# First batch's score tiles as two products of 64 rows each, by halves of the keys

## The chip, the cores and the metric

The kernel runs on one core of one Trainium2 chip, as one launch. The metric is the device time of that launch in microseconds (us), the median of several runs. A shorter time is better.

## The reference

Attention over 4 batches of 8 heads, 576 positions and 64 values a head, all in 32-bit floats, with a threshold in the softmax, and then two feed-forward layers over the 2304 tokens:

```python
scores = scale * np.matmul(q, k.transpose(0, 1, 3, 2))
thresh = np.max(scores, axis=-1, keepdims=True) - tau
scores = np.where(scores >= thresh, scores, -1000000000.0)
scores = scores - np.max(scores, axis=-1, keepdims=True)
attn = np.exp(scores)
attn = attn / (np.sum(attn, axis=-1, keepdims=True) + 1e-09)
return np.matmul(attn, v)                 # then, per token:
x = (s * maximum(x @ w_in, 0)**2 + b) @ w_out
h = x @ w2_in;  out = (maximum(h, 0) + alpha * minimum(h, 0)) @ w2_out
```

A change of the last bits of a score can move a position over the threshold, so the first batch's scores are plain 32-bit products.

## The kernel before

**Stages.** Attention of the first batch comes first (0 to about 131 us in the trace). The weights of the first feed-forward layer are unpacked on DVE, ACT and POOL beside it, and from 80 us on the first layer's products fill TensorE's (PE's) gaps. Then come the other three batches beside the first layer (to about 500 us), and last the rest of both layers.

**Heads.** Heads are taken in pairs. The first batch has four pairs (`p < NP`, `whole`, `first` in `pair`). Of each pair q, k and v are loaded with the two heads side by side, so that after a transposition on PE the 128 partitions are 2 heads x 64 values. A pair has nine score tiles of 128 queries x 576 keys: four for each head, and one with the last 64 queries of both heads (`i == NQ`, the tail). Four pairs make 36 tiles, 32 of one head and 4 tails.

**A score tile before.** PE has 128 rows, a head has 64 values. The scaled queries of a head are written with a factor that is zero on the other head's partitions (`sc_h`, line 676 and 678), so that a product over all 128 rows gives one head. A tile is two products (line 742), keys 0 to 287 and 288 to 575, each into a PSUM bank of its own:

```python
nc.tensor.matmul(sp.t[:, x, :HS], lhsT=o[0][:, c], rhs=o[1][:, x * HS:(x + 1) * HS], ...)
```

The trace shows each 32-bit product as two matmul instructions of 288 columns, each with its weight load, so four to a tile. Then DVE takes the row maxima (`mx`, line 752), POOL the threshold (754), ACT the exponentials (`e`, 756), DVE the masked sum (758); PE transposes `e` by chunks of keys (877, 881), ACT copies these to `gf` and `sh` (887), and PE multiplies them with v (852).

**Moves.** What PE has transposed lies in PSUM and is moved to SBUF: before, six moves a pair, k with 512 and with 64 columns (ACT, 668), q with 512 and with 64 columns for each head (DVE or ACT, 676 and 678).

**Order.** Nothing is ordered by hand. Every piece of work is a task with an engine (or several to choose from), a cost, a rank and its buffers; `Plan.run` plays these costs through once and writes down each engine's instructions in the order in which the tasks start there. On the chip each engine goes through its list in that order. So another cost or another task moves instructions on all engines, far behind its own place too. Two PSUM buffers hold scores (`sc`), one bank (`bank3`, `moe_s`) is shared by the transpositions of pairs 1 to 3 and later by the feed-forward layer.

## Time and profile before

| | |
|---|---|
| Median of three runs | 1115.76 us (1115.6 to 1116.54) |
| Span of the profiled execution | 1111.8 us, from its first to its last instruction |
| Between the two | 3.96 us, before the first and behind the last instruction |
| PE, weight loads, DVE, ACT, POOL busy | 98%, 95%, 82%, 68%, 32% of the span |

The profiled execution is known by its span alone; its time as a run is the span and what lies around it. PE has 98% of the span by the page, but a matmul's record goes on behind the last column that it takes in, so records of neighbours overlap, and the rate of PE is read from one start to the next. The granted clock has 1.00 in every slice of the page; the first 14 us show starts at twice the distance of later ones, as at the lower of the two levels.

### The profile page before, as it was taken

Reading aid. Unit: us, or ns where it says so; the run is one execution under the profiler, and the core shown is the slowest. Engines: PE = TensorE matmul, PEld = TensorE weight load, DVE = VectorE, ACT = ScalarE, POOL = GpSimd, SP = SyncE. Lnnn points to the kernel's source line nnn. Section 1 sums busy time; section 2 is a strip of 40 time slices with the busy share of each in tenths; the row PEclk is TensorE's granted clock in tenths of the full one; section 3 lists DMA queues with packets and bytes.
Section 4 is the critical chain, followed back from the end, with each engine's and each line's share of the span. In section 5 each row is a group of like instructions: output and inputs, shape, how many; then the busy total and the mean of one; then the engine's idle time right before and its main releaser. Section 6 shows DMA issues by size and latency. Waiting matters only on the chain.

```text
span 1111.8 us, 22073 instructions
## 1 busy us (share of the span) xinstructions
PE 1090.6 (98%) x7536; PEld 1051.7 (95%) x7536; DVE 911.6 (82%) x2055; ACT 755.5 (68%) x1737; POOL 352.1 (32%) x476
## 2 busy tenths in 40 slices
PE   8999999999999999999999999999999999999998
PEld 7777899998999999999999999999999999999998
DVE  4898888879888988757877789589986999998882
ACT  4888878867877868744554377357786998565551
POOL 1576764644654646500000013020120332112111
PEclk9999999999999999999999999999999999999999
DMA  5663363446444454044466565428834464554531
GB/s 119 177 167 123 107 168 86 109 118 156 109 118 118 118 124 108 12 139 134 125 217 209 173 205 161 126 86 278 279 132 164 146 211 154 159 160 119 154 90 39
DMA packets 185265, 158.36 MB, mean 142 GB/s; under 512 B 72000, under 2 KB 162112, under 8 KB 185152
## 3 DMA queue, kind: packets, MB, share of 16 engines
q1 hardware_dynamic: 182624, 154.79, 48.6%
q10 hardware_dynamic: 2528, 2.16, 0.7%
q8 instruction: 59, 0.97, 0.3%
q14 instruction: 54, 0.44, 0.1%
HBM read 91.10 MB, written 44.56 MB: 122 GB/s over the span
## 4 chain that ended last, share of the span: by engine, by line
PE 79%; DVE 9%; ACT 5%; DMA 3%; issue 2%; SPq 1%; POOL 0%; DVEq 0%; ACTq 0%; POOLq 0%
PE bank L480 12%; PE bank L481 11%; PE bank L482 11%; PE bank_b L481 8%; PE bank_b L480 8%; PE bank_b L482 8%; PE bank L852 7%; PE sc L742 7%; PE bank L877 5%; ACT e L756 1%; PE bank L881 1%; DVE e L758 1%; PE bank L660 1%; DMA stg<-wfi 1%; DVE mx L752 1%
## 5 line engine op out<-in xcount | busy, mean ns | idle before, releaser
L758 DVE SCALAR_TENSOR_TENSOR e<-sc,mx,e 128x576 f32<-128x576 f32 x144 | 116.3, 813 | 16.8 <-ACT e L756 13.2
L756 ACT ACTIVATE e<-sc,mx 128x576 f32<-128x576 f32 x144 | 106.4, 742 | 21.4 <-DVE mx L752 20.7
L877 PE MATMUL bank<-eyes,e 128*128 128x128 f32 (+1 forms) x640 | 120.2, 274 | 0.6 <-ACT gf L896 0.3
L752 DVE TENSOR_REDUCE mx<-sc 128x1 f32<-128x576 f32 x144 | 107.0, 751 | 13.7 <-PE sc L742 12.8
L877 PEld LDWEIGHTS bank<-eyes,e 128*128 128x128 f32 (+1 forms) x640 | 80.2, 139 | 13.4 <-issue 1.3
L480 PE MATMUL bank<-xt,wa 128*128 128x256 f32 (+1 forms) x266 | 84.3, 317 | 1.9 <-ACT rest L518 1.1
L480 PE MATMUL bank<-gt,wa 128*128 128x256 f32 (+1 forms) x267 | 83.5, 313 | 0.9 <-ACT rest L518 0.7
L481 PE MATMUL bank<-gt,wa 128*128 128x256 f32 (+1 forms) x267 | 78.9, 295 | 0.2 <-DVE gt L458 0.2
L482 PE MATMUL bank<-gt,wa 128*128 128x256 f32 (+1 forms) x267 | 78.9, 295 | 0.0
L754 POOL TENSOR_SCALAR mx<-mx,tau_s 128x1 f32<-128x1 f32 x144 | 51.4, 358 | 83.7 <-DVE mx L752 80.2
L482 PE MATMUL bank<-xt,wa 128*128 128x256 f32 (+1 forms) x266 | 76.8, 289 | 0.0
L481 PE MATMUL bank<-xt,wa 128*128 128x256 f32 (+1 forms) x266 | 76.7, 289 | 0.0
L742 PE MATMUL sc<-k,q 128*128 128x288 f32 x272 | 65.5, 369 | 1.8 <-DVE e L758 0.9
L852 PE MATMUL bank<-gl,vt 128*128 128x256 f32 (+1 forms) x192 | 64.8, 338 | 1.2 <-POOL gl L907 0.6
L852 PE MATMUL bank<-gh,vt 128*128 128x256 f32 (+1 forms) x192 | 57.8, 301 | 0.1
L541 ACT ACTIVATE gt<-rest,b_b,s_b 128x384 fp32r<-128x384 f32 x56 | 39.5, 708 | 26.5 <-DVE rest L539 26.3
L481 PE MATMUL bank_b<-gt,wa 128*128 128x384 f32 (+1 forms) x168 | 54.4, 324 | 1.1 <-DVE gt L531 1.0
L912 DVE TENSOR_TENSOR gl<-bank,gh 128x256 fp32r<-128x256 f32 (+1 forms) x96 | 43.4, 452 | 14.3 <-ACT gh L910 12.8
L480 PE MATMUL bank_b<-gt,wa 128*128 128x384 f32 (+1 forms) x168 | 54.3, 323 | 0.2 <-ACT n L1174 0.2
L480 PEld LDWEIGHTS bank<-xt,wa 128*128 128x128 f32 x266 | 50.4, 189 | 4.1 <-ACT rest L518 2.2
L482 PE MATMUL bank_b<-gt,wa 128*128 128x384 f32 (+1 forms) x168 | 54.1, 322 | 0.0
L922 POOL TENSOR_TENSOR gr<-gf,gh 64x256 fp32r<-64x256 f32 (+1 forms) x48 | 39.7, 828 | 44.2 <-DVE gl L920 43.0
(649 smaller groups left out, 4158.2 us busy)
## 6 DMA issues: line engine op xcount, KB each, us to landing
stg<-in_moe_w_in_dram SPq DMA_DIRECT2D x32, 512.0 KB, 4.0
stg<-in_moe_w_out_dram SPq DMA_DIRECT2D x32, 512.0 KB, 3.7
qo<-hq SPq DMA_DIRECT2D x32, 256.0 KB, 4.3
gf<-rest SPq DMA_DIRECT2D x30, 192.0 KB, 2.3
rest<-gf SPq DMA_DIRECT2D x40, 128.0 KB, 2.9
ko<-hk SPq DMA_DIRECT2D x32, 144.0 KB, 2.7
xr<-xs SPq DMA_DIRECT2D x6, 768.0 KB, 5.2
yf<-yb SPq DMA_DIRECT2D x24, 192.0 KB, 2.6
```

The source lines that it names most:

```text
L480: nc.tensor.matmul(o, lhsT=wl, rhs=mh, start=first, stop=False, skip_group_check=on_top)
L481: nc.tensor.matmul(o, lhsT=wh, rhs=ml, start=False, stop=False, skip_group_check=on_top)
L482: nc.tensor.matmul(o, lhsT=wh, rhs=mh, start=False, stop=last, skip_group_check=on_top)
L742: nc.tensor.matmul(sp.t[:, x, :HS], lhsT=o[0][:, c], rhs=o[1][:, x * HS:(x + 1) * HS], start=n == 0, stop=n == len(passes) - 1)
L752: add("DVE", dve(S), lambda sp=sp, mx=mx: nc.vector.tensor_reduce(mx.t[:, 0:1], sp.t[:, :, :HS], op=ALU.max, axis=AX.XY, negate=True), (sp ...
L754: t2 = add("POOL", 0.26, lambda mx=mx: nc.gpsimd.tensor_scalar(mx.t[:, 1:2], mx.t[:, 0:1], -1.0, tau_s, op0=ALU.mult, op1=ALU.subtract), ( ...
L756: add("ACT", act(S, 1), lambda sp=sp, mx=mx, e=e: nc.scalar.activation(halves(e.t), sp.t[:, :, :HS], AF.Exp, bias=mx.t[:, 0:1]), (sp, mx), ...
L758: add("DVE", dve(S) + 0.065, lambda sp=sp, mx=mx, e=e, col=col, sums=sums: nc.vector.scalar_tensor_tensor(halves(e.t), sp.t[:, :, :HS], mx ...
L852: nc.tensor.matmul(o.t[:, :n], lhsT=w.rearrange("p a b -> p (a b)"), rhs=m.t[:, :n], start=c == first and x == 0, stop=c == last and x == ...
L877: nc.tensor.transpose(gt.t[:rows, m:m + P], es[i].t[:, keys], ident)
L912: add("DVE", dve(n), lambda hi=hi, lo=lo, gt=gt: nc.vector.tensor_tensor(lo.t[:, :n], gt.t[:, :n], f32(hi.t[:, :n]), op=ALU.subtract), (gt ...
L922: add("POOL", pool2(n), lambda hi=hi, f=f, hf=hf: nc.gpsimd.tensor_tensor(hi.t[:TL, :n], f.t[:TL, :n], f32(hf.t[:TL, :n]), op=ALU.subtract ...
```

## The change

The keys of the first batch are kept in two halves of 288, and both queries and keys twice: once with head 0 on partitions 0 to 63 and head 1 on 64 to 127 (index 0), once the other way round (index 1). For a tile of head h the product with the first half of the keys then uses the 64 rows on one half of the array, and that with the second half the 64 rows on the other half. The four tails keep products over 128 rows; for these POOL clears the columns where a head has no queries. The order of the keys within `e` changes (0 to 255, 512 to 575, 256 to 511), and the transpositions of `e` read their chunks accordingly.

The moves from PSUM become thirteen a pair: q with 512 columns at once and two more of 64 partitions, k with 256 columns three times (twice 64 partitions) and with 32 columns three times, and four of 64 columns for the tail's queries. Each of them may go to ACT or DVE.

```diff
--- before.py
+++ after.py
@@ -582,7 +582,9 @@
-        q32, k32 = tiles(ep, NP, "q32", [P, NS * P]), tiles(ep, NP, "k32", [P, S])
+        q32, k32 = tiles(ep, NP, "q32", [P, 2, NK * P]), tiles(ep, NP, "k32", [P, 2, HS])
+        for t in q32:
+            nc.gpsimd.memset(t[:, :, NQ * P:], 0.0)
@@ -602,6 +604,48 @@
+        def twice(p, nat, q_of, k_of, rank):
+
+            n = HS - G1
+            tk, tq, tt = (Buf(one_s, "misc"), Buf(one_s, "gt"), Buf(moe_s)) if p == 0 else (Buf(moe_s), Buf(moe_s), Buf(moe_s))
+
+            def turned(t, tr, cs):
+                for i, c in enumerate(cs):
+                    nc.tensor.transpose(tr.t[:, i * P:(i + 1) * P], t.t[:, c].rearrange("p h d -> p (h d)"), ident)
+
+            def move(o, tr, cols, to, by=None, rows=P):
...
+                add([("ACT", act(w, by is not None), rank), ("DVE", dve(w) + 0.065 * (by is not None), rank)], 0, go, (tr,), (to,))
+
+            every, (lo, hi) = slice(0, P), half(0)
+            add("PE", pe(P, NQ), lambda: turned(nat["k"], tk, range(NQ)), (nat["k"],), (tk, k_of), rank=rank)
+            add("PE", pe(P, NQ), lambda: turned(nat["q"], tq, range(NQ)), (nat["q"],), (tq, q_of), rank=rank)
+            move((q32[p][:, 0, :NQ * P], every), tq, slice(0, NQ * P), q_of, sc_p)
+            move((k32[p][:, 0, :G1], every), tk, slice(0, G1), k_of)
+            for a, b in (lo, hi), (hi, lo):
+                move((k32[p][a, 1, n:], b), tk, slice(G1, 2 * G1), k_of)
+            add("PE", pe(P), lambda: turned(nat["k"], tt, (NQ,)), (nat["k"],), (tt, k_of, q_of), rank=rank)
+            move((k32[p][:, 0, G1:], every), tt, slice(0, n), k_of)
+            for a, b in (lo, hi), (hi, lo):
+                move((k32[p][a, 1, :n], b), tt, slice(n, 2 * n), k_of)
+            for a, b in (lo, hi), (hi, lo):
+                move((q32[p][a, 1, :NQ * P], b), tq, slice(0, NQ * P), q_of, sc_p)
+            for h, b in enumerate((lo, hi)):
+                for x, a in enumerate((b, (hi, lo)[h])):
+                    move((q32[p][a, x, NQ * P + h * TL:NQ * P + (h + 1) * TL], b), tt, slice(TL, P), q_of, sc_p)
@@ -643,8 +687,10 @@
+            if first:
+                twice(p, nat, qs[0], ks[0], ready)
+            for nm in () if first else "kq":
...
@@ -663,22 +709,6 @@
-                    if first:
-                        if nm == "k":
-                            add("ACT", act(n), lambda hl=hl, tr=tr, c=c, n=n: nc.scalar.activation(
-                                k32[p][:, c], tr.t[:, :n], AF.Copy), (tr,), (hl,), rank=ready)
-                            continue
-                        for h in range(2):
...
-                            add([("DVE", dve(n) + 0.065, ready), ("ACT", act(n, 1), ready)], 0, scaled, (tr,), (hl,))
-                        continue
@@ -727,14 +757,19 @@
+                    def by_keys(sp=sp, h=h, c=slice(ii * P, (ii + 1) * P)):
+                        for x in range(2):
+                            r = slice(0, P) if h is None else half(h ^ x)[0]
+                            nc.tensor.matmul(sp.t[:, x, :HS], lhsT=q32[p][r, x, c], rhs=k32[p][r, x], start=True, stop=True)
@@ -743,7 +778,7 @@
-                    add("PE", pe(HS, 8) if first else pe_r(HS, 2 * len(passes)), score, of, (sp,), rank=rank - AHEAD)
+                    add("PE", (pe(HS, 8) if h is None else pe(HS, 4) + 0.1) if first else pe_r(HS, 2 * len(passes)), by_keys if first else score, of, (sp,), rank=rank - AHEAD)
@@ -869,7 +904,10 @@
-                keys = slice(S - rows, S) if c == NQ else slice(c * P, (c + 1) * P)
+                if plain:
+                    keys = slice(G1, G1 + rows) if c == NQ else slice(c * P + TL * (c > 1), (c + 1) * P + TL * (c > 1))
+                else:
+                    keys = slice(S - rows, S) if c == NQ else slice(c * P, (c + 1) * P)
```

In the order of the instructions, ACT from its first move on. Before (`q320`, `k320` are queries and keys of pair 0 in SBUF, `bank0` to `bank3` PSUM banks, `[waits X]` names the engine waited for):

```order
L678 ACTIVATE q320_165<-bank0_105,by_half_77 128x512 [waits DVE_49]
L668 ACTIVATE k320_169<-bank2_107 128x512 [waits PE_49]
L668 ACTIVATE k320_169<-bank3_108 128x64 [waits DVE_49,PE_49]
L756 ACTIVATE e0_137<-sc0_109,mx0_154 128x576 [waits DVE_49]
L756 ACTIVATE e1_138<-sc1_110,mx1_155 128x576 [waits DVE_49]
```

and now:

```order
L627 ACTIVATE q320_165<-bank0_105,sc_p_76 64x512 [waits DVE_49]
L627 ACTIVATE q320_165<-bank0_105,sc_p_76 64x512
L623 ACTIVATE k320_169<-bank2_107 64x256 [waits DVE_49]
L623 ACTIVATE k320_169<-bank2_107 64x256
L627 ACTIVATE q320_165<-bank3_108,sc_p_76 64x64 [waits DVE_49,PE_49,Pool_49]
L627 ACTIVATE q320_165<-bank3_108,sc_p_76 64x64 [waits DVE_49]
L791 ACTIVATE e0_137<-sc0_109,mx0_154 128x576 [waits DVE_49]
L791 ACTIVATE e1_138<-sc1_110,mx1_155 128x576 [waits DVE_49]
```

Six moves of pair 0 stand in front of the first exponential on ACT where three stood.

DVE from the first row maximum on, where the second pair's moves (`q321`, `k321`) fall. Before:

```order
L752 TENSOR_REDUCE mx0_154<-sc0_109 128x1 [waits PE_49]
L752 TENSOR_REDUCE mx1_155<-sc1_110 128x1 [waits PE_49]
L758 SCALAR_TENSOR_TENSOR e0_137,sums0_158<-sc0_109,mx0_154,e0_137 128x576 [waits Activation_49,Pool_49]
L676 TENSOR_SCALAR q321_166<-bank3_108,by_half_77 128x512 [waits PE_49]
L758 SCALAR_TENSOR_TENSOR e1_138,sums0_158<-sc1_110,mx1_155,e1_138 128x576 [waits Activation_49,Pool_49]
L752 TENSOR_REDUCE mx2_156<-sc0_109 128x1 [waits PE_49]
L758 SCALAR_TENSOR_TENSOR e2_139,sums0_158<-sc0_109,mx2_156,e2_139 128x576 [waits Activation_49,Pool_49]
L752 TENSOR_REDUCE mx3_157<-sc1_110 128x1 [waits PE_49]
L676 TENSOR_SCALAR q321_166<-bank3_108,by_half_77 128x64 [waits PE_49,Activation_49]
L758 SCALAR_TENSOR_TENSOR e3_140,sums0_158<-sc1_110,mx3_157,e3_140 128x576 [waits Activation_49,Pool_49]
```

and now:

```order
L787 TENSOR_REDUCE mx0_154<-sc0_109 128x1 [waits PE_49]
L787 TENSOR_REDUCE mx1_155<-sc1_110 128x1 [waits PE_49]
L793 SCALAR_TENSOR_TENSOR e0_137,sums0_158<-sc0_109,mx0_154,e0_137 128x576 [waits Activation_49,Pool_49]
L793 SCALAR_TENSOR_TENSOR e1_138,sums0_158<-sc1_110,mx1_155,e1_138 128x576 [waits Activation_49,Pool_49]
L625 TENSOR_SCALAR q321_166<-bank3_108,sc_p_76 64x512 [waits Activation_49]
L787 TENSOR_REDUCE mx2_156<-sc0_109 128x1 [waits PE_49]
L787 TENSOR_REDUCE mx3_157<-sc1_110 128x1 [waits PE_49]
L621 COPY k321_170<-bank3_108 64x256 [waits Activation_49]
L793 SCALAR_TENSOR_TENSOR e2_139,sums0_158<-sc0_109,mx2_156,e2_139 128x576 [waits Pool_49]
L621 COPY k321_170<-bank3_108 64x32 [waits Activation_49]
L625 TENSOR_SCALAR q321_166<-bank3_108,sc_p_76 64x64 [waits Activation_49] x2
L793 SCALAR_TENSOR_TENSOR e3_140,sums0_158<-sc1_110,mx3_157,e3_140 128x576 [waits Pool_49]
```

Two moves of pair 1 have become five, in the same four tiles.

PE in steady work, a score tile (L742, now L770) among the transpositions of `e` (L877, now L915) and the products with v (L852, now L887). Before:

```order
L852 MATMUL bank2_107<-sh0_145,v320_173 128x256 [waits Pool_49]
L877 MATMUL bank0_105<-eyes_70,e0_137 64x128 [waits Activation_49]
L877 MATMUL bank0_105<-eyes_70,e1_138 64x128
L852 MATMUL bank2_107<-gf1_144,v320_173 128x256
L742 MATMUL sc0_109<-k321_170,q321_166 128x288 [waits DVE_49]
L742 MATMUL sc0_109<-k321_170,q321_166 128x288
L852 MATMUL bank2_107<-sh1_146,v320_173 128x256 [waits Activation_49]
```

and now:

```order
L887 MATMUL bank1_106<-sh0_145,v320_177 128x256 [waits Activation_49,Pool_49]
L614 MATMUL bank3_108<-eyes_70,nat2_132 128x128 [waits DMAHW1_49,DMAHW0_49,Activation_49]
L915 MATMUL bank2_107<-eyes_70,e0_137 128x128
L915 MATMUL bank2_107<-eyes_70,e1_138 128x128
L770 MATMUL sc0_109<-k320_169,q320_165 128x288 [waits DVE_49]
L770 MATMUL sc0_109<-k320_169,q320_165 128x288
L887 MATMUL bank1_106<-gf1_144,v320_177 128x256 [waits Activation_49]
L915 MATMUL bank0_105<-eyes_70,e0_137 64x128
L915 MATMUL bank0_105<-eyes_70,e1_138 64x128
L887 MATMUL bank1_106<-sh1_146,v320_177 128x256 [waits Activation_49]
```

The two score products stand next to each other, and products over 128 rows stand in front and behind. In the whole new order the 32 tiles with half the rows stand in 28 such places.

## Rows read from the trace of the kernel before

**Rows 1.** The page, part 1: busy time, share of the span, instructions.

```profile
PE 1090.6 (98%) x7536; PEld 1051.7 (95%) x7536; DVE 911.6 (82%) x2055; ACT 755.5 (68%) x1737; POOL 352.1 (32%) x476
```

**Rows 2.** Busy time by stretch; the first row names the columns.

```profile
core 0: us, PE busy (x) PEld busy (x) DVE busy (x) ACT busy (x) POOL busy (x), PEclk, DMA share, GB/s
0.00:20.00 20.00, 17.09 (x74) 14.30 (x75) 8.27 (x21) 7.42 (x15) 3.84 (x21) 1.00 0.58 131
20.00:80.00 60.00, 57.54 (x306) 44.07 (x305) 49.72 (x112) 49.24 (x117) 33.99 (x44) 1.00 0.64 166
80.00:140.00 60.00, 59.21 (x360) 48.81 (x360) 52.76 (x110) 50.47 (x108) 41.74 (x47) 1.00 0.39 114
140.00:500.00 360.00, 352.13 (x2837) 343.40 (x2836) 298.27 (x698) 269.17 (x608) 186.74 (x275) 1.00 0.45 114
500.00:1111.80 611.80, 604.63 (x3967) 601.07 (x3966) 502.60 (x1117) 379.19 (x892) 85.82 (x93) 1.00 0.52 160
```

**Rows 3.** PE in order of time, in the middle of the stretch.

```profile
61.33 0.38 PE L877 MATMUL bank<-eyes,e 128*128 128x128 f32 x2
61.55 1.14 PE L742 MATMUL sc<-k,q 128*128 128x288 f32 x4
62.52 0.59 PE L852 MATMUL bank<-gf,v 128*128 128x256 f32 x2
```

**Rows 4.** PE in order of time, from the first score tile on.

```profile
9.57 4.21 PE L742 MATMUL sc<-k,q 128*128 128x288 f32 x8 [0.56 <-ACT k L668]
13.57 1.01 PE L828 MATMUL bank<-eyes 128*128 128x128 f32 x4
...
15.36 1.24 PE L742 MATMUL sc<-k,q 128*128 128x288 f32 x4
```

**Rows 5.** Groups by line and shape, 0 to 140 us: score matmuls, moves, nearest copies.

```profile
L742 PE MATMUL sc<-k,q 128*128 128x288 f32 x160 | 46.2, 415 | 1.1 <-ACT k L668 0.6 <-DVE e L758 0.4
...
L887 ACT ACTIVATE gf<-bank 128x256 f32<-128x256 f32 x16 | 6.2, 387 | 3.2 <-PE bank L877 3.2
...
L814 DVE TENSOR_TENSOR z<-z,bank 128x256 f32<-128x256 f32 x8 | 3.4, 420 | 3.5 <-ACT z L934 3.4
...
L676 DVE TENSOR_SCALAR q<-bank,by_half 128x512 f32<-128x512 f32 x4 | 3.0, 750 | 3.9 <-PE bank L660 3.1 <-ACT q L678 0.7
L678 ACT ACTIVATE q<-bank,by_half 128x512 f32<-128x512 f32 x4 | 2.8, 702 | 7.5 <-DVE q L676 7.0 <-PE bank L660 0.5
...
L668 ACT ACTIVATE k<-bank 128x512 f32<-128x512 f32 x4 | 2.4, 601 | 0.0
...
L678 ACT ACTIVATE q<-bank,by_half 128x64 f32<-128x64 f32 x4 | 1.1, 313 | 1.4 <-DVE q L676 1.4
...
L676 DVE TENSOR_SCALAR q<-bank,by_half 128x64 f32<-128x64 f32 x4 | 1.0, 278 | 0.7 <-PE bank L660 0.7
L668 ACT ACTIVATE k<-bank 128x64 f32<-128x64 f32 x4 | 0.9, 224 | 1.1 <-PE bank L660 1.0
```

**Rows 6.** Line 938, an ACT copy from one half of the partitions to the other.

```profile
L938 ACT ACTIVATE sh<-bank x48: 377/407/437, 143.0 to 478.5; 64x256 f32<-64x256 f32 x24, 64x320 f32<-64x320 f32 x24
```

**Rows 7.** ACT in order of time, the moves before the first score.

```profile
8.35 0.69 ACT L678 ACTIVATE q<-bank,by_half 128x512 f32<-128x512 f32 x1 [6.34 <-DVE q L676]
8.93 0.92 ACT L668 ACTIVATE k<-bank 128x512 f32<-128x512 f32 x2
```

**Rows 8.** DVE in order of time, the same stretch.

```profile
7.56 0.75 DVE L676 TENSOR_SCALAR q<-bank,by_half 128x512 f32<-128x512 f32 x1 [3.09 <-PE bank L660]
9.05 0.47 DVE L676 TENSOR_SCALAR q<-bank,by_half 128x64 f32<-128x64 f32 x2 [0.74 <-PE bank L660]
```

**Rows 9.** Waits of 20 to 140 us: total, times, longest.

```profile
DVE e L758 <- ACT e L756: 4.5, 7, 1.1
DVE mx L752 <- PE sc L742: 4.5, 11, 0.9
```

**Rows 10.** Line 480: first and last start of the feed-forward products.

```profile
L480 PE MATMUL bank<-xt,wa x266: 277/283/525, 80.7 to 896.7; 128*128 128x256 f32 x116, 128*128 128x384 f32 x17
```

More of the change, by code (lines that the diff above doesn't have):

```diff
@@ L603, in half, with go @@
             return (slice(0, D), slice(D, P)) if h == 0 else (slice(D, P), slice(0, D))
+        def twice(p, nat, q_of, k_of, rank):
[5 more added lines that the diff above has]
+            def move(o, tr, cols, to, by=None, rows=P):
+                def go(e, o=o):
+                    d, r = o
+                    if by is None:
+                        if e == "DVE":
+                            nc.vector.tensor_copy(d, tr.t[r, cols])
+                        else:
+                            nc.scalar.activation(d, tr.t[r, cols], AF.Copy)
+                    elif e == "DVE":
+                        nc.vector.tensor_scalar(d, tr.t[r, cols], by[r], None, op0=ALU.mult)
+                    else:
+                        nc.scalar.activation(d, tr.t[r, cols], AF.Copy, scale=by[r])
+                w = cols.stop - cols.start
+                add([("ACT", act(w, by is not None), rank), ("DVE", dve(w) + 0.065 * (by is not None), rank)], 0, go, (tr,), (to,))
[15 more added lines that the diff above has]
+                    move((q32[p][a, x, NQ * P + h * TL:NQ * P + (h + 1) * TL], b), tt, slice(TL, P), q_of, sc_p)
@@ L645, in pair @@
             qk, ends = {}, ((sc_h[0], slice(NQ * P, S)), (sc_h[1], slice(S, S + TL)))
-            for nm in "kq":
-                t, hl = nat[nm], (ks if nm == "k" else qs)[0] if first else Buf(hk_s if nm == "k" else hq_s)
+            if first:
+                twice(p, nat, qs[0], ks[0], ready)
+            for nm in () if first else "kq":
+                t, hl = nat[nm], Buf(hk_s if nm == "k" else hq_s)
                 qk[nm] = hl
@@ L655, in pair @@
                     else:
-                        tr = Buf(one_s, {"k": "misc", "q": "gt"}[nm]) if p == 0 and not tail else Buf(moe_s) if whole else Buf(one_s, "misc")
+                        tr = Buf(one_s, "misc")
                         def transpose(t=t, tr=tr, cs=(NQ,) if tail else tuple(range(NQ))):
@@ L729, in pair @@
                     if first:
[L730 removed]
+                        of, passes = (qs[0], ks[0]), ()
                     elif h is None:
@@ L735, in pair, with score @@
                         of, passes = (qs[h], ks[h]), [(qs[h], 1, ks[h], None), (qs[h], 0, ks[h], None)]
-                    def score(sp=sp, passes=passes, c=slice((col if first else ii) * P, ((col if first else ii) + 1) * P)):
+                    def by_keys(sp=sp, h=h, c=slice(ii * P, (ii + 1) * P)):
+                        for x in range(2):
+                            r = slice(0, P) if h is None else half(h ^ x)[0]
+                            nc.tensor.matmul(sp.t[:, x, :HS], lhsT=q32[p][r, x, c], rhs=k32[p][r, x], start=True, stop=True)
+                    def score(sp=sp, passes=passes, c=slice(ii * P, (ii + 1) * P)):
                         for n, o in enumerate(passes):
```

8 lines of the change are left out of this document (1 added, 7 removed).

## The prediction

> **What bounds the kernel now.** I read the busy shares first: PE 98%, DVE 82%, ACT 68%, POOL 32% [rows 1]. A share is a mean over stages, so next the busy time by stretch [rows 2]. From 20 to 140 us, where the first batch runs, PE is busy 57.54 + 59.21 = 116.75 of 120 us, DVE 49.72 + 52.76 = 102.48, ACT 49.24 + 50.47 = 99.71. PE is the bound there with 3.25 us of waits, and DVE is a near second with 17.5 us to spare. Behind it PE stays the bound: 352.13 of 360 us, then 604.63 of 611.8. So what PE saves in the first batch is passed on to the end, since the work behind it is PE's too; from 80.7 us on feed-forward products already stand ready to fill PE [rows 10]. The first 20 us are different: PE has 17.09, DVE 8.27 and ACT 7.42, and there the chain from load to first score decides.
>
> In order of time, a score tile starts at 61.55 and the next product at 62.52: 0.97 us for four matmul instructions, 0.243 each [rows 3]. Its record is 1.14 long, so 0.17 us of tail lie behind the last column taken in. A tile whose weight load started only with it has a record of 1.24 in place of 1.14 [rows 3, 4]: a bare weight load is 0.10 us. The first two tiles run at the lower of TensorE's two levels: eight instructions from 9.57 to 13.57, 0.50 each [rows 4], though the stretch has 1.00 as granted clock [rows 2].
>
> **The change part by part.**
>
> *Score tiles.* 32 of 36 become two products of 64 rows, on different halves of the array. No instruction goes away: two 32-bit products of 288 columns are still four matmul instructions. All the gain is in how far the two run at once, and the trace has no matmul with half the rows (the score group is 128*128 throughout [rows 5]). Bounds for one tile, from rows: two fully abreast, half of 0.97, 0.49 us; nothing abreast, and at both changes of shape the tail of 0.17 and a bare load of 0.10, 0.97 + 2 x 0.27 = 1.51. That is -0.48 to +0.54 us a tile, over 32 tiles -15.4 to +17.3 us.
>
> I take a value between. A product's two instructions need the same 64 rows, so the second waits for the first, and the second product stands behind both in PE's list. If PE starts matmuls in the order of its list, only the last instruction of the first product and the first of the second run together: three steps of 0.243, 0.73 us. I add one bare load of 0.10, for weights that can't be loaded while other shapes occupy the rows. That is 0.83, 0.14 less than 0.97, and nearer to the row of today's tile than to either end: 32 x 0.14 = 4.5 us less on PE.
>
> The Trainium skill ("TensorE: Matmul & The Clock Gate", The mechanism) says that matmuls on different row groups start about 4 ns apart, and that matmuls start and end in the order of the program; the first half by itself would make a tile 0.49 us, both together give the three steps. No run here shows either yet.
>
> *Moves.* Before, a pair has six: 0.60 + 0.22 for k, 2 x 0.73 + 2 x 0.30 for q (means of the DVE and ACT rows), 2.88 us [rows 5]. Now thirteen. Time goes by columns, not partitions: a copy of 64 partitions with 256 columns from one half to the other is 0.377 at its shortest, one over 128 is 0.387 [rows 5, 6], so crossing halves costs nothing. Three scaled ones of 512 are 3 x 0.73 = 2.18, three of 256 columns 3 x 0.39 = 1.17 (on DVE about 0.42, line 814), three of 32 at most as those of 64, 3 x 0.22 = 0.67, four scaled of 64 are 4 x 0.30 = 1.18: 5.20 us. Four pairs: 4 x 2.32 = 9.3 us more, about 4.7 us on each of DVE and ACT. Most of it hides behind PE. But DVE would then have 107.2 of 115.5 us (120 less the 4.5), and its spare time falls from 17.5 to 8.3. PE's 3.25 us of waits grow; I charge half as much again, 1.6 us. If the cover is gone altogether the price is one engine's 4.7, if PE never notices it is nothing. Waits of today between these engines are small: DVE waits 4.5 us for exponentials and 4.5 for scores [rows 9], and a sooner score shortens the second.
>
> *Start.* ACT issues one move of 0.69 from 8.35 and two of k until 9.85 [rows 7], DVE its first from 7.56 [rows 8]. Now ACT has two scaled ones (1.4) and two of 256 columns (0.8) from 8.35, until about 10.5; the first tile's second product needs the last of these. Its first product can start near 9.5, with 0.96 us at the lower level, so the second starts about where it would in any case. The first tile ends where it did, near 11.5, the second up to 0.5 us sooner. Bounds: 0.7 later (10.5 against 9.85), 0.5 sooner; I take nothing. Two moves of pair 1 that become five fall on DVE between row maxima, 0.3 to 0.8 us each; that is in the 1.6.
>
> *At nothing.* Four clearings on POOL fall into the first 20 us, where it is busy 3.84 with 21 instructions [rows 2]; uncovered, at their mean of 0.18, they would cost 0.7. The other order of the keys moves no instruction. Tails stay as they are. The new order behind 140 us moves work everywhere without making any; I take 0, and 2 us to either side as its bounds, a fifth of PE's idle 7.9 us of 140 to 500.
>
> *Sum.* -4.5 + 1.6 = -2.9 us. The profiled span is 1111.8; with 3.96 us around it that execution stands for the median of 1115.76. 1111.8 - 2.9 + 3.96 = **1112.9 us**.
>
> **The rivals.**
>
> 1. *Both products fully abreast.* The four instructions take two steps and a bare load, 0.49 + 0.10 = 0.59: 32 x 0.38 = 12.2 us off PE. For it: the tile's products write two PSUM banks and read different partitions, so nothing shared is seen. Against: PE's rows show strict succession everywhere. DVE would have 107.2 us in 107.8, so some 4 of the 12 come back as waits: -8, **1107.8**.
>
> 2. *Changes of shape cost more than the overlap gives* (the other side). A score tile stands between products over 128 rows; in the new order the 32 tiles stand in 28 such places, so PE changes shape 56 times. If each waits out the tail of 0.17, a tile is 0.73 + 0.34 = 1.07, 32 x 0.10 = 3.2 us more, and with the 1.6 of the moves +4.8; if each has the bare load too, 0.73 + 0.54 = 1.27, +9.6 + 1.6 = +11.2. Time 1120.5 to 1127, middle **1122**. It decides from 0.92 us a tile on, where 32 x 0.05 only pays the 1.6: that is 0.19 us for the two changes. For it: a tail and a bare load can be read in the rows. Against: both are hidden between all other shapes of today, such as 128 and 288 columns [rows 3]. The Trainium skill ("TensorEngine Tiling (Array Packing)", Key Properties) speaks for this rival: changing the tiling mode drains TensorE, changing the tile alone does not. No run here shows such a change yet.
>
> 3. *The change doesn't do what it says:* the halves run one after the other at 0.97. Then only the moves count: +1.6, **1117.4**. Against it: they use different rows.
>
> 4. *PE gains, but the vector engines hand none of it on,* because in the first 20 to 40 us pair after pair waits for 13 moves through one bank: 4.5 saved, 4.7 lost, **1116**. For it: ACT's wait for DVE's move of q is 7.0 us [rows 5], nearly all of it at the start. Against: PE's 57.54 of 60 us.
>
> **How the numbers follow.** Forecast 0.36, rival 1 0.25, rival 2 0.20, rival 3 0.09, rival 4 0.10. The likeliest's own range is 1110 to 1115. The range: up to 1121 it takes in rivals 3 and 4 and the lower part of rival 2, leaving out about 0.12; down to 1106 nearly all of rival 1, leaving out 0.06. About 0.2% (2.2 us) is what a measurement of this kernel can tell from no change. Faster than 1113.5: rival 1's 0.25 and 0.27 of the forecast's 0.36, 0.52. Within 1113.5 to 1118: 0.09 of the forecast and 0.13 of rivals 3 and 4, 0.22. Slower: rival 2's 0.20 and 0.06 of rivals 3 and 4, 0.26.
>
> **What would show it.** The score rows of the first batch must read 64*128; from a tile's first start to the start of the next product is 0.83 (0.59: rival 1; 1.07 or more: rival 2; 0.97: rival 3). Starts within a tile tell the overlap: third start with the second is mine, third with the first is rival 1. The groups of the moves should add up to about 21 us where there were 11.5. In 20 to 140 us PE's waits should grow from 3.25 to about 5; if they grow by as much as PE saves, it was rival 4. I am wrong if the tile is shorter and the span isn't, or if a later stretch moves by more than 2 us.

## The result and the profile after

The changed kernel takes 1127.34 us (median of 4 runs, 1125.95 to 1128.1) against 1115.68 of the kernel before on the same chip: a ratio of 1.0103, interval 1.0089 to 1.0117, so 11.7 us slower. Forecast were 1112.9 and a range up to 1121. Its profiled execution is the run of 1125.95, with a span of 1124.2 us.

The page's first part answers to [rows 1]:

```profile
PE 1091.2 (97%) x7536; PEld 1037.0 (92%) x7536; DVE 923.5 (82%) x2078; ACT 750.7 (67%) x1737; POOL 353.0 (31%) x485
```

The busy time of DVE rose by 11.9 us, and that of PE did not fall. By stretch, for [rows 2]:

```profile
core 0: us, PE busy (x) PEld busy (x) DVE busy (x) ACT busy (x) POOL busy (x), PEclk, DMA share, GB/s
0.00:20.00 20.00, 14.27 (x78) 10.51 (x78) 9.84 (x26) 9.72 (x20) 5.00 (x25) 1.00 0.58 131
20.00:80.00 60.00, 51.51 (x264) 32.62 (x263) 52.57 (x113) 46.05 (x110) 25.09 (x33) 0.94 0.54 138
80.00:140.00 60.00, 57.53 (x338) 41.70 (x336) 49.72 (x105) 49.02 (x104) 38.63 (x45) 1.00 0.41 119
140.00:500.00 360.00, 351.54 (x2797) 339.06 (x2797) 297.45 (x694) 266.19 (x609) 198.06 (x289) 1.00 0.46 112
500.00:1124.20 624.20, 616.37 (x4068) 613.12 (x4066) 513.88 (x1143) 379.72 (x897) 86.18 (x94) 1.00 0.52 160
```

From 20 to 140 us PE is busy 109.04 us, where it was 116.75, so it stands idle 10.96 us where it stood 3.25. That isn't a gain: the work of the first batch ends later, and the first feed-forward product, which [rows 10] have at 80.7, starts at 94.0.

```profile
L480 PE MATMUL bank<-xt,wa x268: 277/283/520, 94.0 to 915.8; 128*128 128x256 f32 x116, 128*128 128x384 f32 x18
```

PE in order of time shows the new score tile (start, length, idle time ahead), to be set against [rows 3]:

```profile
22.62 0.76 PE L770 MATMUL sc<-k,q 64*128 64x288 f32 x4
23.31 0.70 PE L887 MATMUL bank<-gf,v 128*128 128x256 f32 x2
```

From the tile's start to the next product's it is 0.69 us, before 0.97. The records of the single instructions show how: of one tile, two start at 63.278 and 63.285, the other two at 63.625 and 63.632. Two instructions on the same 64 rows start 0.24 us apart where nothing runs abreast (`e16`, below), so each of these pairs has one instruction of either product: the two products run fully abreast.

Most of the 0.28 is lost again at the two changes of shape. Ahead of the tile 0.09 us more pass than elsewhere (shown below). Behind it the first of the next product's two instructions takes 0.32 us, before 0.215; in the rows that product has 0.70, where [rows 3] have 0.59. From the last instruction ahead of a tile to the second one behind it, where nothing waits, 1.21 us pass where 1.30 passed: 0.09 us less a tile, some 3 us over 32.

The Trainium skill ("TensorE: Matmul & The Clock Gate", The mechanism) has matmuls on different rows start some 4 ns apart, and the 7 ns are near that. It also has matmuls start in the order of the program; that can't be read here, since a record doesn't tell which product it belongs to.

The moves by line and shape, 0 to 140 us (count | busy us, mean ns | idle time ahead and what ended it), answer to [rows 5]:

```profile
L770 PE MATMUL sc<-k,q 64*128 64x288 f32 x128 | 25.3, 470 | 2.2 <-DVE e L793 1.8 <-DVE k L621 0.3
...
L627 ACT ACTIVATE q<-bank,sc_p 64x512 f32<-64x512 f32 x6 | 4.1, 682 | 8.1 <-DVE q L625 8.0
...
L627 ACT ACTIVATE q<-bank,sc_p 64x64 f32<-64x64 f32 x9 | 2.8, 309 | 2.4 <-DVE q L625 2.3
...
L623 ACT ACTIVATE k<-bank 64x256 f32<-64x256 f32 x6 | 2.3, 377 | 0.8 <-DVE k L621 0.8
...
L625 DVE TENSOR_SCALAR q<-bank,sc_p 64x64 f32<-64x64 f32 x7 | 2.0, 284 | 3.0 <-ACT q L627 3.0
```

All 14 groups of moves add up to 20.4 us, where there were 11.2. ACT's wide moves wait 8.0 us for DVE's moves of the same queries, but 7.0 of that was there before [rows 5], nearly all of it ahead of the first score. New are the waits of the small moves: DVE's wait 3.0 us for ACT's and ACT's 2.3 for DVE's, where ACT's had waited 1.4 and DVE's none for ACT. One bank's moves go to and fro. The waits of 20 to 140 us (total, times, longest) answer to [rows 9]:

```profile
PEld bank L887 <- ACT gf L925: 10.8, 14, 1.6
...
PE bank L887 <- ACT gf L925: 6.1, 8, 1.3
DVE e L793 <- ACT e L791: 4.6, 7, 1.7
...
DVE mx L787 <- PE sc L770: 3.8, 8, 0.8
```

The two waits of [rows 9] are as they were. New is the first: PE's weight loads (PEld) for the products with the values wait 10.8 us for ACT's copies of the transposed weights (`gf`), before 2.0; PE itself waits 6.1 us for them, before 0.6. Such a row of PEld has to be read with care. Behind a 64-row tile, where nothing else waits, the weight loads stand still for 0.385 us each time (before: 0.05), and the view puts that down to whatever was signalled last (ACT's `e`, `z`, `wa` or `gf`, or nothing). In the changed kernel 4 of the 14 waits for `gf` stand behind a tile, and the other 10 make 8.0 us, so here most of it is waiting for ACT.

### The profile page after: what moved, and what is told of

Its sections match the earlier page's. It is cut to its first block, busy times and chain, and to the rows that moved or that the text cites. A ratio compares the mean times of both kernels' runs of the same rounds, so it can differ in the third digit from the quotient of the medians.

```text
span 1124.2 us, 22112 instructions
## 1 busy us (share of the span) xinstructions
PE 1091.2 (97%) x7536; PEld 1037.0 (92%) x7536; DVE 923.5 (82%) x2078; ACT 750.7 (67%) x1737; POOL 353.0 (31%) x485
## 4 chain that ended last, share of the span: by engine, by line
PE 77%; DVE 9%; ACT 7%; DMA 3%; issue 2%; SPq 1%; POOL 1%; DVEq 0%; ACTq 0%
PE bank L480 11%; PE bank L481 11%; PE bank L482 11%; PE bank_b L481 8%; PE bank_b L480 8%; PE bank_b L482 8%; PE bank L887 6%; PE bank L915 5%; PE sc L777 4%; PE sc L770 1%; ACT e L791 1%; PE bank L919 1%; DVE mx L787 1%; DVE e L793 1%; DMA stg<-xs 1%
## 5 line engine op out<-in xcount | busy, mean ns | idle before, releaser
L915 PE MATMUL bank<-eyes,e 128*128 128x128 f32 (+1 forms) x640 | 121.4, 276 | 3.3 <-DVE e L793 0.8
L791 ACT ACTIVATE e<-sc,mx 128x576 f32<-128x576 f32 x144 | 106.0, 742 | 11.7 <-DVE mx L787 10.7
L915 PEld LDWEIGHTS bank<-eyes,e 128*128 128x128 f32 (+1 forms) x640 | 79.7, 139 | 20.6 <-ACT gf L941 1.7
L480 PE MATMUL bank<-gt,wa 128*128 128x256 f32 (+1 forms) x258 | 79.8, 309 | 0.2
L481 PE MATMUL bank<-gt,wa 128*128 128x256 f32 (+1 forms) x258 | 76.0, 294 | 0.3 <-DVE gt L458 0.3
L482 PE MATMUL bank<-gt,wa 128*128 128x256 f32 (+1 forms) x258 | 75.9, 294 | 0.0
L789 POOL TENSOR_SCALAR mx<-mx,tau_s 128x1 f32<-128x1 f32 x144 | 47.0, 327 | 87.7 <-DVE mx L787 75.2
L887 PE MATMUL bank<-gl,vt 128*128 128x256 f32 (+1 forms) x192 | 65.6, 342 | 0.7 <-POOL gl L945 0.6
L887 PE MATMUL bank<-gh,vt 128*128 128x256 f32 (+1 forms) x192 | 58.2, 304 | 0.9 <-DVE z L977 0.6
L481 PE MATMUL bank_b<-gt,wa 128*128 128x384 f32 (+1 forms) x177 | 57.4, 324 | 1.0 <-DVE gt L531 1.0
L480 PE MATMUL bank_b<-gt,wa 128*128 128x384 f32 (+1 forms) x177 | 57.3, 324 | 0.5 <-ACT gt L530 0.5
L482 PE MATMUL bank_b<-gt,wa 128*128 128x384 f32 (+1 forms) x177 | 57.1, 323 | 0.0
L480 PEld LDWEIGHTS bank<-xt,wa 128*128 128x128 f32 x268 | 50.7, 189 | 6.2 <-ACT rest L518 3.6
L538 ACT ACTIVATE rest<-bank 128x384 f32<-128x384 f32 x38 | 18.6, 489 | 50.9 <-PE bank L482 50.9
L481 PEld LDWEIGHTS bank<-xt,wa 128*128 128x128 f32 x268 | 50.9, 190 | 0.2
```

The lines of the kernel that those rows point to most:

```text
L480: nc.tensor.matmul(o, lhsT=wl, rhs=mh, start=first, stop=False, skip_group_check=on_top)
L481: nc.tensor.matmul(o, lhsT=wh, rhs=ml, start=False, stop=False, skip_group_check=on_top)
L482: nc.tensor.matmul(o, lhsT=wh, rhs=mh, start=False, stop=last, skip_group_check=on_top)
L789: t2 = add("POOL", 0.26, lambda mx=mx: nc.gpsimd.tensor_scalar(mx.t[:, 1:2], mx.t[:, 0:1], -1.0, tau_s, op0=ALU.mult, op1=ALU.subtract), ( ...
L791: add("ACT", act(S, 1), lambda sp=sp, mx=mx, e=e: nc.scalar.activation(halves(e.t), sp.t[:, :, :HS], AF.Exp, bias=mx.t[:, 0:1]), (sp, mx), ...
L887: nc.tensor.matmul(o.t[:, :n], lhsT=w.rearrange("p a b -> p (a b)"), rhs=m.t[:, :n], start=c == first and x == 0, stop=c == last and x == ...
```

## The experiments

Two theories of the loss stood at first. M: pairs of heads wait for 13 moves that two engines hand to and fro. O: the planner, given 0.59 us for a score tile, lists ACT's copies badly. Each run is compared with the kernel before on its own chip.

**Price, moves, handing over.** Four kernels. `e1` plans the changed kernel at the old price; `e2` gives the kernel before 7 repeated moves a pair; `e4` is the changed kernel with a bank's moves on one engine; `e5` makes the second copies of pairs 1 to 3 by DMA, from the first ones.

```diff
e1, against the changed kernel:
-add("PE", (pe(HS, 8) if h is None else pe(HS, 4) + 0.1) if first ...
+add("PE", (pe(HS, 8)) if first ...
e2, against the kernel before, after each move of k and of a q tail:
+for r, s0_, w in (...): add([("ACT", act(w), ready), ("DVE", dve(w), ready)], 0, again, (tr,), (hl,))
e4, against the changed kernel ("ACT" for the two wide moves of q):
-add([("ACT", ...), ("DVE", ...)], 0, go, (tr,), (to,))
+add([(only, us, rank)], 0, lambda: go(only), (tr,), (to,))
e5, against the changed kernel, pairs 1 to 3:
+hwdge(lambda a=a, b=b: nc.sync.dma_start(k32[p][a, HS:], kn.t[b, :HS]), (kn,), (k_of,), rank, 74)
+hwdge(lambda a=a, b=b: nc.sync.dma_start(q32[p][a, 1], q32[p][b, 0]), (q_of,), (), rank, 164)
```

> The changed kernel (1127.3 us), with one number of the planner put back: a half-row score tile is planned with 0.98 us as before, not 0.59. Same instructions, another order. Theory M (thirteen moves a pair, handed to and fro between ACT and DVE, hold up the next pair's scores; order is secondary): 1124 to 1130. Theory O (the plan, which takes score tiles for cheaper than they are, puts ACT's copies of the transposed e behind other work): 1110 to 1117.

> The kernel before (1115.7 us), score tiles of 128 rows, with moves written a second time to where they already go: each pair has three more of 256 columns, two of 32 and two of 64, thirteen in all, about 2.2 us a pair more on ACT and DVE together. Theory M: 1121 to 1129. Theory O (moves hide behind PE): 1115 to 1118.

> The changed kernel with the engine of each move fixed: those from the bank of q's 512 columns on ACT, all others on DVE, so that no chain of moves passes from one engine to the other and back. Theory M with the handing over as its cause: 1117 to 1123. Theory M with the sheer number of moves as its cause: 1125 to 1131. Theory O: 1125 to 1130.

> The changed kernel, but for pairs 1 to 3 the second copies (q and the second half of k on the other partitions) are made by DMA: four DMAs and six moves a pair in place of thirteen moves; keys stay in their natural order; pair 0 has twelve moves. Score tiles still overlap. Theory M: 1106 to 1114, below the kernel before. Theory O: 1121 to 1128. If the DMAs come late behind the loads on their queue: 1116 to 1122 with waits of PE for DMAs before 45 us.

Measured: `e1` 1128.7 us (1.012, 1.0101 to 1.0139), so the old price alone doesn't bring the time back. `e2` 1123.8 (1.0077, 1.0062 to 1.0092), `e4` 1122.4 (1.0062, 1.0047 to 1.0077): both fit M. `e5` 1126.2 (1.0101, 1.0071 to 1.0131), though ACT and DVE make fewer moves: M fails there, and O's range holds it. In all four the planner lists the work anew, and that turned out to matter.

**TensorE's part alone, and the order alone.** A third theory joins here. V: the chain of the vector engines (row maximum, exponential, masked sum) sets the end of the first batch, and TensorE's time is covered by it. `e6` is the kernel before with 64-row products from the data that lies there, without the copies; it leaves out the scores of the second half of the keys. `e7` and `e8` make the tiles of both heads together, one on each half of the rows, without copies; `e8` with one wide move of q instead of two. `e3` changes nothing but the price.

```diff
e6, against the kernel before (price as in the changed kernel):
+r = slice(0, P) if h is None else half(h ^ x)[0]
+nc.tensor.matmul(sp.t[:, x, :HS], lhsT=q32[p][r, c], rhs=k32[p][r, x * HS:(x + 1) * HS], start=True, stop=True)
e7:
+for x in range(2):
+    for h, o in zip((1, 0), sps):
+        nc.tensor.matmul(o.t[:, x, :HS], lhsT=q32[p][r, ...], rhs=k32[p][r, x * HS:(x + 1) * HS], ...)
e8, besides:
-for h in range(2):
+for h in range(2 if tail else 1):
e3:
-add("PE", pe(HS, 8) if first ...
+add("PE", (pe(HS, 8) if i == NQ else pe(HS, 4) + 0.1) if first ...
```

> The kernel before with its own moves and layout (6 wide moves a pair, none added), but each first-batch score tile is two products of 64 rows, one on each half of the partitions, planned at the changed kernel's price. The second product of a tile meets zeros in the queries, so the scores of the second half of the keys are left out. Theory M (the second copies and their handing to and fro eat what TensorE saves): with no copies to wait for, TensorE's 0.28 us a tile are handed on, so 32 x 0.28 = 9 us at most and some 5 us at least come off: 1106 to 1111 us, and TensorE's waits before 140 us stay near the 12.8 us of the kernel before. Theory V (in the first batch the end of each tile is set by the chain of the vector engines, row maximum, exponential, masked sum, so that TensorE's time there is cover): 1113 to 1117 us, TensorE's waits before 140 us grow by 6 to 9 us to some 20.

> The kernel before with its own moves and layout, but the score tiles of the two heads are made together: four products of 64 rows, one head's on the lower and the other head's on the upper half of the partitions, both halves of the keys each, so that two tiles take about 1.4 us as in the changed kernel and no second copy is needed. The price is that both score buffers must be free at once, and the turns of the heads alternate. Theory M: no copies to wait for, 1107 to 1112 us. Theory V: 1114 to 1118 us, or more where the two tiles at once leave the vector engines without work at each pair's start.

> As the one with the two heads' tiles made together, and the wide move of the queries is one instead of one for each head, since 64-row products need no zeros in the other half: 4 wide moves of some 0.65 us fewer than in the kernel before. Theory M, by which a move between the turn of the keys and the pair's first score is on the path: 2 to 3 us below the two heads abreast with two moves, so 1105 to 1110 us. Theory V, by which the vector engines set the end of the first batch: also below it, by the 2.6 us of work halved over two engines or more, so 1112 to 1117 us.

> The kernel before, every instruction of it, but the plan prices the 32 first-batch score tiles at 0.59 us instead of 0.98, so only the order on the engines differs. It tells how much of a difference is the order alone. Theories M and V both expect little, 1113 to 1119 us. If the order by itself is worth more than 5 us, a theory of the order (the plan that the new price makes is the worse one) is alive again, though the changed kernel planned at the old price was no faster.

Measured: `e6` 1123.6 us (1.0077, 1.0056 to 1.0098), `e7` 1137.8 (1.0208, 1.0181 to 1.0235), `e8` 1138.2 (1.021, 1.0185 to 1.0234), `e3` 1126.5 (1.0108, 1.0079 to 1.0138). None of the four falls in a range that M or V had set. The last upsets the rest: with every instruction as it was, the kernel is as slow as the changed one. Its busy time by stretch:

```profile
20.00:140.00 120.00, 115.83 (x653) 91.48 (x652) 102.10 (x214) 99.92 (x221) 68.80 (x84) 1.00 0.50 137
140.00:500.00 360.00, 347.77 (x2747) 333.54 (x2746) 290.75 (x683) 261.89 (x594) 196.39 (x286) 1.00 0.44 109
```

Against [rows 2] PE is busy 0.92 us less from 20 to 140 and 4.36 less from 140 to 500, where the attention of the other three batches lies. The last masked sum of all batches comes at 479.5 us, where it came at 466.3; that of the first batch comes sooner, at 122.1 for 123.7. So this loss arises behind the first batch. `e7` and `e8` are slower than any new order was; the two score buffers that must be free together may be why (in `e7` DVE waits 10.6 us for scores from 20 to 140, before 4.5), but no run splits it from their order.

**How much an order is worth.** The kernel before at four more prices of the 32 tiles (0.97, 1.00, 1.04, 0.96 in place of 0.98), and the changed one at two (0.69, 0.75 in place of 0.59). Theory R: the order of the kernel before is a lucky one, and nearly any other loses. Theory P: only the far price of 0.59 makes a bad order.

```diff
-add("PE", pe(HS, 8) if first ...
+add("PE", (pe(HS, 8) if i == NQ else 0.97) if first ...
```

> The kernel before, every instruction of it, with the plan's price of the 32 first-batch score tiles at 0.97 us, which is what the trace shows, instead of 0.98. The order of the engines' lists comes out differently almost everywhere for that hundredth. Theory R (the kernel before has an order that is better than what the planner makes for nearly any other numbers, and any edit that makes it plan anew loses it): 1119 to 1128 us, though nothing is slower in it. Theory P (only the far price of 0.59 makes a bad plan; near prices plan as well as before): 1113 to 1117 us.

> The same with the price at 1.00 us, two hundredths above the one before. Theory R: 1119 to 1128 us. Theory P: 1113 to 1117 us. The three of the kernel before at other prices (0.59, 0.97, 1.00) tell how far the time moves by the order alone.

> The changed kernel, every instruction of it, planned with the score tile at the 0.69 us that its trace shows instead of 0.59. Theory R: the changed kernel moves by several us to either side from one price to the next, 1118 to 1130 us. Theory M (the copies handed to and fro hold the scores up in any order): 1125 to 1130 us, as at 0.59 and 0.98.

> The same with the price at 0.75 us. Theory R: 1118 to 1130 us, and away from the run at 0.69 by some us. Theory M: 1125 to 1130 us. The mean of the changed kernel over its prices against the mean of the kernel before over its new prices is what the instructions themselves are worth: theory R expects the two means within 3 us of each other, theory M the changed kernel's higher by 4 us or more.

> The kernel before with the plan's price of the 32 score tiles at 1.04 us. A fourth sample of what a new order is worth with nothing else changed. Theory R: 1116 to 1127 us, as the three so far (1116.3, 1122.2, 1126.5), and not below the 1115 of the kernel before. Theory P: 1113 to 1117 us.

> The same with the price at 0.96 us, a fifth sample. Theory R: 1116 to 1127 us. Theory P: 1113 to 1117 us.

| price | kernel before, us (ratio) | price | changed kernel, us (ratio) |
|---|---|---|---|
| 0.96 | 1115.9 (1.001, 1.000 to 1.002) | 0.59 | 1127.3 (1.0103) |
| 0.97 | 1122.2 (1.0071, 1.0048 to 1.0095) | 0.69 | 1123.9 (1.0077, 1.0062 to 1.0092) |
| 1.00 | 1116.3 (1.001, 1.0001 to 1.0019) | 0.75 | 1123.7 (1.0076, 1.006 to 1.0091) |
| 1.04 | 1119.2 (1.0038, 1.0022 to 1.0054) | 0.98 | 1128.7 (1.012) |
| 0.59 | 1126.5 (1.0108) | | |

A hundredth of a microsecond in one price moves the same instructions by 7 us. None of five new orders beats the one before, and two lie only 0.1% above it; their mean ratio is 1.0047. P falls, since 0.97 and 1.04 are near prices and lose 7 and 4 us. R holds in part: its ranges miss 1.00 and 0.96. The changed kernel's mean over four orders is 1.0094. The two means lie 0.0047 apart, 5.2 us, which by the expectation of `e12` speaks for M (4 us or more) and not for R (within 3): beside the order, the changed kernel's own instructions cost something. `e1` to `e8` differ by less than such orders do (`e7` and `e8` apart), so they settle nothing by themselves.

**The order held.** What was needed is the change without a new order. These three kernels keep the planner's numbers, so every list stands row for row as before, and the edits are made inside the rows: the 64-row products (`e13`), the moves in 13 pieces (`e14`), and the whole change, layout and clearings too (`e15`).

```diff
e13, against the kernel before, at its price:
+nc.tensor.matmul(sp.t[:, x, :HS], lhsT=q32[p][r, c], rhs=k32[p][r, x * HS:(x + 1) * HS], start=True, stop=True)
e14 (and q's second wide move and tails in two halves):
-nc.scalar.activation(k32[p][:, c], tr.t[:, :n], AF.Copy)
+for r, s1 in (slice(0, P), 0), (slice(0, D), w), (slice(D, P), w):
+    nc.scalar.activation(k32[p][r, c0 + s1:c0 + s1 + w], tr.t[r, s1:s1 + w], AF.Copy)
e15, the same places, into the changed kernel's layout:
+nc.scalar.activation(k32[p][:, 0, d:d + w], tr.t[:, :w], AF.Copy)
+for a, b in half(0), half(1):
+    nc.scalar.activation(k32[p][a, 1, lo:hi], tr.t[b, w:2 * w], AF.Copy)
```

> The kernel before with its own price and so its own lists on every engine, row for row; only the products of the 32 first-batch score tiles read 64 rows each, so that a tile takes TensorE 0.69 us, not 0.97. No copies are added; the second product of a tile meets zero queries, so the scores of the second half of the keys are left out. With the order held, this is what TensorE's 9 us are worth by themselves. Theory R (the order made the loss, the saving is real): 1106 to 1111 us. Theory V (the vector engines' chain sets the first batch's end, TensorE's time in it is cover): 1113 to 1116 us, with TensorE's waits up by what its work lost.

> The kernel before with its own price and lists, score tiles of full rows, and each pair's 6 moves made in 13 pieces of the changed kernel's shapes, by the engine and at the place where the list of the kernel before has the one move. With the order held and no handing over between engines inside a bank, this is what the moves are worth by themselves. Theory R: the pieces cost their own 9 us on two engines with 10 to 15% idle, 1115 to 1118 us. Theory M: each pair waits for the moves, 1119 to 1124 us.

> The changed kernel's layout, its 13 moves a pair, its clearings and its 64-row products, all at the places that the lists of the kernel before have for them (each move's pieces on the engine that had the one move). The whole change with the order held. Theory R: the sum of the two others, saving and moves, 1108 to 1116 us, faster than or level with the kernel before. Theory M: 1120 to 1127 us as the changed kernel. Theory V: 1115 to 1120 us, the moves' cost and no saving.

Measured: `e13` 1114.4 us (0.9999, 0.9989 to 1.0008), `e14` 1120.1 (1.005, 1.0032 to 1.0069), `e15` 1118.0 (1.0031, 1.0018 to 1.0045). When the n-th masked sum of DVE starts, one for each score tile, shows where (us, from the traces; the 36th is the first batch's last, the 144th that of all four):

| tile | before | e13 | e14 | e15 | e3 | changed |
|---|---|---|---|---|---|---|
| 1st | 14.5 | 12.6 | 15.7 | 14.9 | 13.9 | 13.1 |
| 10th | 41.7 | 42.2 | 47.9 | 47.2 | 37.5 | 45.4 |
| 36th | 123.7 | 123.1 | 129.5 | 127.6 | 122.1 | 129.8 |
| 144th, last | 466.3 | 465.8 | 473.0 | 470.0 | 479.5 | 479.0 |

From the 36th to the last it is 342.6 us before, 342.4 in `e15` and 349.2 in the changed kernel. So the changed kernel loses 6.1 us in the first batch and 6.6 behind it, and `e15` loses only the first sort.

`e13`, which leaves out the scores of the second half of the keys, has its first tile 1.9 us sooner; from the 10th on it is within 0.6 us of before. Its tiles are short (PE in order of time):

```profile
61.64 0.38 PE L882 MATMUL bank<-eyes,e 128*128 128x128 f32 x2
61.95 0.76 PE L740 MATMUL sc<-k,q 64*128 64x288 f32 x4
62.64 0.70 PE L857 MATMUL bank<-gf,v 128*128 128x256 f32 x2
```

A tile takes 0.69, the two transposes ahead of it 0.31 where [rows 3] have 0.22 (61.33 to 61.55), and the product behind it 0.70 where they have 0.59. That leaves 0.09 us a tile, some 3 us of TensorE. The waits for ACT's copies seem to take them back:

```profile
PEld bank L857 <- ACT gf L892: 4.5, 11, 0.7
...
PEld bank L857 <- ACT sh L892: 3.9, 8, 0.9
```

Each was 2.0 before. But 10 of these 19 stand behind a 64-row tile, 9 of them with just the 0.385 us of the change of shape; the other nine make 1.7 and 2.8 us, little more than before. Where the saving goes can be seen in one place, at the start of a pair. Before, PE and ACT have:

```profile
29.70 0.66 PE L660 MATMUL bank<-eyes,nat 128*128 128x128 f32 x4 [0.63 <-ACT q L678]
```

```profile
29.34 0.31 ACT L678 ACTIVATE q<-bank,by_half 128x64 f32<-128x64 f32 x1 [1.41 <-DVE q L676]
```

and in `e13`:

```profile
29.77 0.66 PE L660 MATMUL bank<-eyes,nat 128*128 128x128 f32 x4 [2.19 <-ACT q L678]
```

```profile
29.40 0.31 ACT L678 ACTIVATE q<-bank,by_half 128x64 f32<-128x64 f32 x1 [2.68 <-DVE q L676]
```

PE's score tile ahead of it starts 1.1 us sooner (26.82 for 27.94) and is shorter, and PE waits 1.6 us longer for a move that comes when it came. From the 10th to the 36th tile, with most moves done, `e13` gains 1.1 us, about half of what its 22 tiles of 64 rows save there (22 x 0.09 = 2.0). In 20 to 140 us ACT and DVE do what they did, in the same time (for the columns see [rows 2]):

```profile
20.00:140.00 120.00, 113.42 (x664) 80.51 (x662) 102.61 (x223) 99.28 (x224) 75.09 (x88) 1.00 0.52 140
```

`e14` loses by the 10th tile nearly all that it loses (6.2 us; 6.7 at the last), in the 45 us in which the moves lie. From 0 to 50 us:

```profile
PEld bank L660 <- ACT q L682: 2.4, 2, 1.5
PEld sc L746 <- ACT k L670: 2.2, 1, 2.2
```

They were 1.1 and 1.0 before. `e15` pays nearly as much for the moves (5.5 us at the 10th tile), and with them in place the shorter tiles do give something back: against `e14` it is 0.7 us ahead at the 10th tile, 1.9 at the 36th, 3.0 at the last, and 2.2 by the medians. Of the ranges set before, `e13` and `e15` fall in V's and `e14` in M's. But V's reason, that TensorE's time is covered, holds only in part: some of it is handed on.

**Fewer moves.** With the order held, `e16` reads both products of a tile from its own head's 64 rows; then one wide move of q a pair does for two.

```diff
against the kernel before, at its price:
+if not tail and h:
+    return
...
+r = slice(0, P) if h is None else half(h)[0]
```

> The lists of the kernel before, with fewer moves, not more: the score tile of one head reads only that head's 64 rows (both products on the same rows, so no overlap is asked for inside a tile), so the queries of both heads need one wide move a pair instead of two; the second is left out where it stood, 4 in all, some 0.65 us each on the row-scaling engine. Output and tiles as in the kernel before. Theory V (the vector engines' chain sets the first batch's end; with the order held, 28 pieces more cost 5.2 us): 2.6 us less of work on that chain, most of it handed on, 1112 to 1114 us, faster than both kernels. Theory T (only TensorE's own time or the order count): 1115 to 1116 us.

Measured: 1126.6 us (1.0106, 1.0089 to 1.0123). Both expectations miss, since I had let TensorE's time stand at 0.97. Its rows:

```profile
69.58 0.38 PE L885 MATMUL bank<-eyes,e 128*128 128x128 f32 x2
69.89 1.24 PE L743 MATMUL sc<-k,q 64*128 64x288 f32 x4
71.05 0.70 PE L860 MATMUL bank<-gf,v 128*128 128x256 f32 x2
```

The tile takes 1.16, the transposes ahead 0.31 and the product behind 0.70: together 0.39 us more than in [rows 3], 32 x 0.39 = 12.5 us. Nothing runs abreast here, so this is the price of two changes of shape. Part of it is passed on: from the 10th masked sum (48.6 us) to the 36th (136.9) `e16` falls back by 6.3 us against before, where the tiles between put 22 x 0.39 = 8.6 on PE.

The other part of the loss has another cause in this trace. Until about 26.7 us starts lie at twice the distance, as at the lower of the two levels, though the granted clock has 1.00 there:

```profile
16.07 2.29 PE L743 MATMUL sc<-k,q 64*128 64x288 f32 x4
...
20.72 2.29 PE L743 MATMUL sc<-k,q 64*128 64x288 f32 x4
```

Before, such starts end at 14 us. By the 10th masked sum `e16` is 6.9 us behind, and it is 12.5 behind at the last. Whether the later rise belongs to the change, no run shows.

From 20 to 140 us PE has 118.75 of 120 us, and DVE waits 12.6 us for scores where it had waited 4.5 [rows 9]:

```profile
DVE mx L760 <- PE sc L743: 12.6, 17, 2.2
```

```profile
20.00:140.00 120.00, 118.75 (x589) 83.97 (x587) 93.50 (x200) 92.42 (x207) 65.87 (x77) 1.00 0.46 128
```

No version beats the kernel before. The best form of the change is `e15`, some 8 us faster than the changed kernel and 3 slower than before; `e13` is level, but without half of those scores.

## Why the prediction was wrong

*The new order, 0 and 2 to either side.* This is the term that failed by most: it measured some 8 us. From `e15` to the changed kernel the ratio goes from 1.0031 to 1.0103 with the same products and moves; only their order and the engines that the moves go to differ. The same instructions of the kernel before lose 1 to 12 us by a new order. By the masked sums 2.2 us of it lie in the first batch and 6.8 behind it, so both signs of being wrong came true: the tile is shorter and the span isn't, and a later stretch moves by more than 2 us. What makes one order worse than another stays open. So does the share of two things inside the 8 us: the handing over inside a bank (`e4`, which stops it, has a new order too), and the fall of TensorE's clock in the changed kernel (last section), 5.60 us at half the rate and so at most 2.8 us; `e15` has no such stretch from 20 us on.

*What PE saves is passed on to the end.* This step failed too, and the sum's -4.5 with it. I read PE's 116.75 of 120 us as the bound. `e13` takes some 3 us off PE and moves the end by -1.2 to +0.9 us (ratio 0.9989 to 1.0008). Against `e14`, `e15` hands on about 2 of the same 3. The first batch hangs on both: PE's list, and the moves and copies of ACT and DVE that its next instruction needs, are nearly equally long. More on the moves counts (`e14`), and less on PE counts in part. A 97% busy engine didn't say that.

*The score tile.* 0.83 forecast, 0.14 less than before; 0.09 less measured. Rival 1's sign, the two products starting together, is what the trace shows, so the overlap was undersized: fully abreast it is worth 0.48 a tile. The changes of shape were undersized more: one bare load of 0.10 in the sum, 0.39 us in `e16`. That is between rival 2's two cases (0.34 and 0.54 a tile); in the changed kernel the overlap just outweighs it. The Trainium skill ("TensorEngine Tiling (Array Packing)", Key Properties) says a change of tiling mode drains the engine; `e16`'s 0.39 agrees with that.

*The moves.* 9.3 us more of them forecast, 9.2 measured (20.4 less 11.2). The charge of 1.6 was mis-sized: 5.2 by the medians of `e14`, above my bound of 4.7. I spread them over 20 to 140 us, where DVE had 17.5 us to spare; they lie in the first 45 us, ahead of each pair's first scores.

*Start.* Taken as nothing; `e14`'s first tile is 1.2 us late, `e13`'s 1.9 soon. *Clearings:* not run apart from the rest; `e15` holds them and is not above the moves alone.

So of 11.7 us some 8 are the order; the change proper is 5.2 for the moves less about 2 that the shorter tiles give back. Rival 4 had the price of the moves nearly right, 4.7 us for the 5.2 of `e14`, at a chance of 0.10; that PE hands none of its gain on isn't so in `e15`. No rival had a price for the order.

## What to carry to other kernels

Where a planner with priorities makes the lists, time a few plans of the unchanged kernel first: that spread is the noise against which an edit is read, and an edit is tested with the lists held fixed. An engine that is 97% busy in a stretch may still only be level with a chain of other engines; before counting a saving, ask what the instruction behind it waits for. Work added ahead of the first consumer of each stage is on the path however idle its engine is on the whole. And before a wait is believed, look whether it has the same length wherever the shape changes, whoever is named for it.
